# Attention followed by a mixture of experts on one core: how first and second layers are given out beside the attention steps

## The chip, the cores and the metric

The kernel runs on one core of a Trainium2 chip. The metric is the device time of one execution in microseconds (us). Before the change the median of three runs was 1072.3 us (1069.99 to 1074.8).

A core has five engines with an instruction stream of their own, each executed in order: TensorE (PE) for matrix products, VectorE (DVE), ScalarE (ACT), GpSimd (POOL) and SyncE (SP). They wait for one another through semaphores. SP and POOL issue nearly all DMA transfers. Matrix products are written to PSUM, from which DVE or ACT read them; everything else is held in SBUF.

## The reference

Two stages. The first is causal sliding-window attention with a distance bias (`q`, `k`, `v` are 8 batches x 8 heads x 576 tokens x 64):

```
scores = scale * q @ k.T                       # per batch and head
mask   = (rel >= 0) & (rel < 128)              # rel = query position - key position
scores = where(mask, scores - slope[h] * |rel|, -1e9)
attn   = softmax(scores);  x = attn @ v        # x: 4608 tokens x 512
```

The second is a dense mixture of 8 experts on the 4608 rows of `x`:

```
logits = x @ w_gate;  P = exp(logits - logits.max())
8 times: P /= P.sum(1) + 1e-9;  P /= P.sum(0) + 1e-9;  P *= 4608 / 8
out = sum over e of  P[:, e] * (relu(x @ w1[e]) @ w2[e])     # 512 -> 1024 -> 512
```

The gate needs all tokens before `P` is known, but the two layers of an expert need only the tokens of one group. So experts 0 and 1 are computed while the attention runs, and their results wait in `acc16` until `P` is there.

## The kernel before

**Attention in steps.** A batch has 576 tokens, five query blocks of 128 (`NQB`, the last one with 64). A step is (batch b, query block kb, half hf): four heads of one block. There are 8 x 5 x 2 = 80 steps. Each has four pieces:

- `scores` (L319): four products of 64 rows (head size) into `psS`, of which there is one buffer. Two heads lie in rows 0 to 63 and 64 to 127 of `QT` and `KT`, so these products use half of PE's rows each. Then on DVE a predicated copy (L338, not for kb = 0), which folds the window's two key blocks into one, and four bias-and-minimum operations (L349) that read `psS` out; on ACT four exponentials (L360).
- `normed` (L370): on DVE the reciprocal of the sums (L373, L377) and a multiplication (L378).
- `turned` (L385): four transposes on PE (L392) into `psT` (one buffer), a copy to SBUF on ACT (L401), and on DVE a masked copy `pto` (L415) and, once per block, the difference `dV` of two value blocks (L408).
- `values` (L423): value products (L437, L448) into `psX` (one buffer). Each writes 64 of PE's columns, two heads beside each other. After the second half ACT writes the block into `xT` (L457).

In iteration n of the main loop the pieces belong to different steps: scores of step n, `normed` of n-1, `turned` of n-2, `values` of n-3. `front` calls a piece with a priority raised by 600, so that the planner, which orders the instructions of DVE, ACT, POOL and SP, prefers it. PE's order is the order of the program (`manual_schedule`).

**Work between the pieces.** `run_fill(1)` puts one unit of the experts' work on PE. A unit is either a first layer (`l1_tile`, L191: 4 products of 384 columns, evicted by ACT at L198) or a whole second layer of a block of 128 tokens (`l2_tile`, L206: 8 products of 512 columns, evicted by DVE at L475). A job (expert e, token group g of 384) has eight of the one and three of the other. `woven` deals the second layers of the job before among the first layers of the next. An iteration calls `run_fill(1)` three times: behind the scores, behind the transposes, behind the values. First layers alternate between two `psh` buffers, second layers between two `psy` buffers.

**What comes in.** Rows of `q` and `k` come in per batch by POOL's queue (`load_qk`, L266), 576 KB each in short pieces; DVE permutes them (`spread`, L273), SP writes them to DRAM (L283), and two transposing transfers (`stage`, `turn`, L289 and L290) bring them back as `QT` and `KT`. `ahead` says at which step `spread` of the batch bb is called, and `early` at which step `load_qk(bb + 1)` is; `load_v` brings the values in block by block. Loads on POOL's queue are held behind a marker (L589) that waits for the newest block of `xT`. For batch 2 the order is `load_qk(2)` at step (1,0,0), `spread(2)` and `stage(2)` at (1,2,0), and in the same step's second half `load_qk(3)`.

**Behind the attention.** `gate` (L464) runs at the end of each batch. The normalisation of `P` (L711 to L739, DVE and POOL) begins when the last gate is there. Meanwhile PE works off the remaining jobs (L757 to L758), then experts 2 to 7 run in loops that the change does not touch.

Of the kernel before, what the change touches and what calls it, by code (L numbers as in the profile page):

```python
# [12 lines left out]
FP32 = mybir.dt.float32  # L13
# [3 lines left out]
def kernel(  # L17
# [10 lines left out]
    nc = tc.nc  # L28
# [5 lines left out]
    HD = H * Dh  # L34
# [150 lines left out]
    def new_hs(e, g):  # L185
        return [t[:, i, :] for t in h_tiles(per, "h", f"h_{e}_{g}") for i in range(4)]

    def l1_tile(e, ft, hs, t0, c0, c1, ps_pool, bufs=2):
# [9 lines left out]
        recent["act"] = nc.scalar.activation(  # L198
            out=hs[ft][:, c0:c1], in_=psh[:, c0:c1], func=AF.Relu
        )  # L200

    def l2_tile(e, blk, hs, ps_pool, bufs):
        psy = ps_pool.tile([P, HD], FP32, name=f"psy_{e}_{blk}", tag="psy", bufs=bufs)
        ms = blk % BG
        for ft in range(NFT):
            nc.tensor.matmul(  # L206
                out=psy,
                lhsT=hs[ft][:, P * ms : P * ms + P],
                rhs=w2ts[e][ft],
                start=(ft == 0),  # L210
                stop=(ft == NFT - 1),
            )
        return psy

    def woven(l1, l2):
        k = 0
        for i, u in enumerate(l1):
            if i % 2 == 0 and i > 0 and k < len(l2):
                yield l2[k]
                k += 1  # L220
            yield u
        yield from l2[k:]

    aps_scope = ExitStack()
    aps = aps_scope.enter_context(tc.tile_pool(name="aps", bufs=1, space=bass.MemoryType.PSUM))
    with tc.tile_pool(name="asb", bufs=1) as asb:
# [51 lines left out]
        def load_qk(b):  # L278
            nats[b] = [load_rows(q, b), load_rows(k, b)]
# [190 lines left out]
                    )  # L470
            nc.vector.tensor_copy(out=P_sb[:, b0:b1, :], in_=psG[:, 0 : b1 - b0, :])

        def l2_early(e, blk, hs):
# [12 lines left out]
        def early_job(e, g):  # L486
            hs = new_hs(e, g)
            return (
                [lambda ft=ft: l1_tile(e, ft, hs, GT * g, 0, GT, aps) for ft in range(NFT)],
                [lambda ms=ms: l2_early(e, BG * g + ms, hs) for ms in range(BG)]  # L490
                if g < NG - 1 or e == 0
                else hs,
            )

        jobs: list = []

        ready: list = []
        owed: list = []

        def run_fill(n):  # L500

            while n > 0:
                if not ready:
                    if jobs:
                        l1, l2 = early_job(*jobs.pop(0))
                        ready.extend(woven(l1, owed))
                        owed[:] = l2
                    else:
                        return
                ready.pop(0)()  # L510
                n -= 1

        new_T(0)

# [55 lines left out]
        t_next = v_next = 0  # L570
        for n in range(len(steps) + 3):
            lag = 1 if n < 2 else 2
            if n == 1:
# [3 lines left out]
            if n < len(steps):  # L577
# [7 lines left out]
                with ExitStack() as pin:  # L585
# [7 lines left out]
                    if hf == 1 and b + 1 < B and kb > 0:  # L593
                        load_v(b + 1, kb - 1)
                        if kb == NQB - 1:
                            load_v(b + 1, kb)
            front(scores, n)
            run_fill(1)
            front(normed, n - 1)
            if t_next <= n - lag:  # L600
                front(turned, t_next)
                t_next += 1
            run_fill(1)
            if v_next > n - lag - 1:
                continue
            front(values, v_next)
            run_fill(1)
            b, kb, hf = steps[v_next]
            v_next += 1
            if hf == 0:  # L610
                continue
            if b == 0 and kb < BG:
                ready += [
                    lambda ft=ft, kb=kb: l1_tile(0, ft, hs00, 0, P * kb, P * kb + P, aps)
                    for ft in range(NFT)
                ]
                ready.append(lambda kb=kb: l2_early(0, kb, hs00))
            done = b * S + min(S, (kb + 1) * P)
            while (g0 + 1) * GT <= done:

# [5 lines left out]
                jobs.append((1, 0))  # L626
            if kb == NQB - 1:
                g1 = S * (b + 1) // P
                gate(gate_done, g1)
                gate_done = g1  # L630

# [122 lines left out]
        if p < 2:  # L754
            nc.sync.dma_start(out=xps[2, p][:, 3:7, :], in_=slab(p))
    load_w2(2)
    while jobs or ready:  # L757
        run_fill(1)  # L758
    aps_scope.close()

# [343 lines left out]
```

## Time and profile before

| what | value |
|---|---|
| median of three runs | 1072.3 us |
| the profiled execution | 1069.8 us, span 1068.0 us |
| PE busy | 1022.8 us (96%) |
| DVE, ACT, POOL busy | 748.3, 657.9, 487.8 us |
| granted TensorE clock, mean | 0.994 |
| attention: first scores to last gate | 11.9 to 341.4 us |
| remaining jobs of experts 0 and 1 | 341.3 to 386 us |
| experts 2 to 7 | 386.6 us to the end |

PE is counted as busy from a product's start to its modelled end, and neighbouring products overlap in the records; how long a piece really holds PE is read from the starts of consecutive pieces. A wait is the idle time of an engine before an instruction, put down to what ended it. Times inside the trace count from the start of the span.

### The profile page before, as it was taken

To read this page: it belongs to the slowest core of one execution; us is meant where nothing else is said; L and a number is where in the kernel's file an instruction comes from. 1 tells how busy PE (TensorE), PEld (TensorE's weight loads), DVE (VectorE), ACT (ScalarE), POOL (GpSimd) and SP (SyncE) were. 2 spreads that over 40 slices of the span, in tenths; PEclk is the share of its full clock that TensorE was granted. 3 is DMA by queue.
4 is the path that set the end of the run, shared out by engine and by line. 5 is a ranking of instruction groups with operands and counts; after the bars stand their busy time and mean duration, and the time that the engine had idled before them with its cause. 6 is when DMAs were issued, how large, how long until landed. Compare 5 with 4: busy or idle time off the path is not lost.

```text
span 1068.0 us, 21178 instructions
## 1 busy us (share of the span) xinstructions
PE 1022.8 (96%) x7604; PEld 646.2 (61%) x7604; DVE 748.3 (70%) x1988; ACT 657.9 (62%) x1903; POOL 487.8 (46%) x420
## 2 busy tenths in 40 slices
PE   3788999999999989999999999999999999999998
PEld 2443444444445544555577777777777777777775
DVE  5886888887886866765466755775677657665565
ACT  4785877877876356664555555556555555555552
POOL 5321222111110200000677777777777877676760
PEclk9998999999999999999999999999999999999999
DMA  9999999524201944413432252315331452214443
GB/s 180 207 176 140 168 165 137 61 28 63 19 2 50 289 98 97 151 52 100 117 77 98 73 144 71 104 55 150 84 101 56 120 116 60 97 52 155 140 141 129
DMA packets 141258, 115.49 MB, mean 108 GB/s; under 512 B 73568, under 2 KB 130912, under 8 KB 141152
## 3 DMA queue, kind: packets, MB, share of 16 engines
q1 hardware_dynamic: 77664, 82.93, 26.4%
q0 software_dynamic: 63488, 31.21, 23.8%
q8 instruction: 59, 0.97, 0.4%
q14 instruction: 47, 0.39, 0.1%
HBM read 109.28 MB, written 25.95 MB: 127 GB/s over the span
## 4 chain that ended last, share of the span: by engine, by line
PE 81%; DVE 7%; ACT 5%; DMA 3%; issue 2%; POOL 1%; ACTq 0%; POOLq 0%; DVEq 0%
PE a L929 18%; PE psP L785 17%; PE psV L785 8%; PE psh L191 8%; PE psy L206 8%; PE b L929 7%; PE z L883 6%; PE psW L785 4%; ACT pc L360 2%; DMA acc<-in_k_dram 2%; PE psS L332 1%; DMA kT<-k 1%; PE psT L392 1%; PE psX L437 1%; DVE ts L349 1%
## 5 line engine op out<-in xcount | busy, mean ns | idle before, releaser
L191 PE MATMUL psh<-xT,w 128*128 128x384 f16 (+1 forms) x832 | 161.2, 321 | 7.5 <-ACT h L198 6.5
L929 PEld LDWEIGHTS <-h 128*128 128x128 f16 x1392 | 136.1, 98 | 50.0 <-POOL h L858 0.4
L806 ACT COPY psW<-psP 128x384 f32<-128x384 f32 x143 | 66.2, 463 | 148.5 <-PE psP L785 147.6
L857 POOL TENSOR_TENSOR xT<-h,h 128x768 f16<-128x768 f16 x58 | 95.1, 1640 | 120.8 <-DVE h L764 109.6
L785 PE MATMUL psP<-x,xT 128*128 128x384 f16 x576 | 140.6, 326 | 1.8 <-ACT u L770 1.5
L785 PE MATMUL psP<-x,w 128*128 128x384 f16 x576 | 140.7, 326 | 0.9 <-ACT h L198 0.6
L198 ACT ACTIVATE h<-psh 128x384 f16<-128x384 f32 (+1 forms) x208 | 93.4, 463 | 77.1 <-PE psh L191 75.9
L785 PEld LDWEIGHTS <-w 128*128 128x128 f16 x1152 | 112.6, 98 | 45.1 <-issue 2.3
L360 ACT ACTIVATE pc<-ts,nm 128x128 f16<-128x128 f32 (+1 forms) x320 | 124.9, 395 | 20.3 <-DVE nm L349 17.4
L206 PE MATMUL psy<-w,h 128*128 128x512 f16 x552 | 131.2, 380 | 2.5 <-DVE acc L475 2.2
L589 POOL COPY mark_sb<-xT 1x1 f16<-1x1 f16 x75 | 21.9, 293 | 235.9 <-ACT xT L457 229.5
L692 DVE SCALAR_TENSOR_TENSOR acc<-a,P_sb,acc 128x512 f32<-128x512 f32 x87 | 65.1, 748 | 85.3 <-PE a L929 85.3
L764 DVE CUSTOM_DVE_ANT_0 h<-psV,u 128x384 f16<-128x384 f32 x144 | 79.6, 553 | 58.2 <-PE psV L785 46.8
L785 PEld LDWEIGHTS <-xT 128*128 128x128 f16 x864 | 84.5, 98 | 39.1 <-issue 6.4
L929 PE MATMUL a<-xT 128*128 128x256 f16 x696 | 104.4, 273 | 0.0
L191 PEld LDWEIGHTS <-w 128*128 128x128 f16 x832 | 68.8, 99 | 55.6 <-issue 19.2
L858 POOL TENSOR_TENSOR h<-h 128x768 f16<-128x768 f16 x58 | 97.8, 1685 | 4.5
L859 POOL TENSOR_TENSOR xT<-h,xT 128x768 f16<-128x768 f16 x58 | 99.3, 1713 | 0.0
L855 POOL TENSOR_TENSOR s_sb<-h,xT 128x768 f16<-128x768 f16 x58 | 95.2, 1642 | 4.2
L940 DVE SCALAR_TENSOR_TENSOR acc<-a,P_sb,acc 128x256 f32<-128x256 f32 x174 | 82.8, 476 | 14.1 <-PE a L929 14.1
L929 PE MATMUL a<-w,h 128*128 128x256 f16 x636 | 91.7, 273 | 0.1
L883 PE MATMUL z<-w,h 128*128 128x512 f16 x360 | 90.6, 379 | 0.0
(96 smaller groups left out, 1951.1 us busy)
## 6 DMA issues: line engine op xcount, KB each, us to landing
x<-x SPq DMA_DIRECT2D x34, 1344.0 KB, 6.4
w<-in_moe_w_dram POOLq DMA_DIRECT2D x32, 512.0 KB, 7.2
out_dram<-acc SPq DMA_DIRECT2D x36, 256.0 KB, 2.0
x<-xT SPq DMA_DIRECT2D x8, 768.0 KB, 7.7
V<-in_v_dram POOLq DMA_DIRECT2D x32, 128.0 KB, 6.5
acc<-in_q_dram POOLq DMA_DIRECT2D x7, 576.0 KB, 8.7
acc<-in_k_dram POOLq DMA_DIRECT2D x7, 576.0 KB, 13.8
q<-acc SPq DMA_DIRECT2D x7, 576.0 KB, 4.2
```

Source lines behind the costliest of these rows:

```text
L191: nc.tensor.matmul(out=psh[:, c0:c1], lhsT=w1ts[e][dt][:, P * ft : P * ft + P], rhs=xT[:, dt, t0 + c0 : t0 + c1], start=(dt == 0), stop=(d ...
L198: recent["act"] = nc.scalar.activation(out=hs[ft][:, c0:c1], in_=psh[:, c0:c1], func=AF.Relu)
L206: nc.tensor.matmul(out=psy, lhsT=hs[ft][:, P * ms : P * ms + P], rhs=w2ts[e][ft], start=(ft == 0), stop=(ft == NFT - 1),)
L360: nc.scalar.activation(out=pc[0:nq, hh, :], in_=ts[0:nq, hh, :], func=AF.Exp, scale=-1.0, bias=nm[0:nq, hh : hh + 1], accum_out=den[0:nq, ...
L785: nc.tensor.matmul(out=ps, lhsT=a[:, kt, i, :], rhs=x[:, kt, :], start=start and kt == 0, stop=stop and kt == KH - 1, skip_group_check=True,)
L855: nc.gpsimd.tensor_tensor(out=s4, in0=a12, in1=s2, op=ALU.subtract)
L857: nc.gpsimd.tensor_tensor(out=s3, in0=a11, in1=a21, op=ALU.subtract)
L858: nc.gpsimd.tensor_tensor(out=a21, in0=a21, in1=a22, op=ALU.add)
L859: nc.gpsimd.tensor_tensor(out=s2, in0=a22, in1=s3, op=ALU.subtract)
L883: nc.tensor.matmul(out=psy, lhsT=hs(ft)[:, lo : lo + P], rhs=w2ts[e][ft], start=(ft == 0), stop=(ft == NFT - 1),)
L929: nc.tensor.matmul(out=ps, lhsT=a[ft], rhs=x[:, ft, :], start=start and ft == 0, stop=ft == NFT // 2 - 1, skip_group_check=True,)
L940: nc.vector.scalar_tensor_tensor(out=o, in0=ps, scalar=P_sb[:, blk, e : e + 1], in1=o, op0=ALU.mult, op1=ALU.add,)
```

## The change

It touches the attention part alone. The number and shapes of the products do not change: 577,536 columns of first- and second-layer products are issued before experts 2 to 7, in both kernels.

1. Second layers are issued in two halves of four products each (`l2_early` with `half`), into one `psy` buffer; the eviction follows the second half.
2. First layers and halves stand in two queues. `run_unit` takes a half when enough first layers lie behind it (`behind`) and `share`, which grows by 0.75 with each first layer and falls by 1 with each half, has reached a bound.
3. From step 10 on (`lead`, the end of batch 0's ten steps), `run_fill(fill)` gives out columns and not units: 0.96 x (8 x 4 x 384 + 3 x 8 x 512) / 11 = 2145 columns a call, with what was overdrawn kept in `count["left"]`. Before step 10 a call runs one unit, and a further half where one is open.
4. The third call stands before the value products, no longer behind them; and from step 10 on the scores of step n + 1 are issued directly behind the value products of iteration n, with no unit between.
5. `front` raises the priority only for steps below 10.
6. `gate` is called in the next iteration, behind its first fill.
7. `spread(3)` moves from step (2,0,0) to (2,1,0) and `load_qk(4)` with it, from (2,0,1) to (2,1,1); `load_qk(3)` moves from (1,2,1) to (1,4,0).

```diff
-            psy = l2_tile(e, blk, hs, aps, 2)
+        def l2_early(e, blk, hs, st, half):
+            if half == 0:
+                st.append(aps.tile([P, HD], FP32, name=f"psy_{e}_{blk}", tag="psy", bufs=2))
+            psy = st[0]
+            lo = P * (blk % BG)
+            for ft in range(NFT // 2 * half, NFT // 2 * (half + 1)):
+                nc.tensor.matmul(
...
+            if half == 0:
+                return
             recent["dve"] = nc.vector.tensor_copy(
...
+        def run_unit(half=False):
+            if not firsts_q and jobs:
+                start_job(*jobs.pop(0))
+            late = half or (
+                halves_q
+                and count["run"] >= halves_q[0][0]
+                and count["share"] >= (2 if count["whole"] else 1)
+            )
+            if halves_q and (late or not firsts_q):
+                halves_q.pop(0)[1]()
+                count["share"] -= 1
+                return NFT // 2 * HD
+            if firsts_q:
+                firsts_q.pop(0)()
+                count["run"] += 1
+                count["share"] = min(count["share"] + 0.75, 2.0)
+                return NDT * GT
+            return 0
         def run_fill(n):
...
+            if count["whole"]:
+                if run_unit() and halves_q and len(halves_q) % 2:
+                    run_unit(True)
+                return
+            count["left"] += n
+            while count["left"] > 0:
+                done = run_unit()
+                if not done:
+                    count["left"] = 0.0
+                    return
+                count["left"] -= done
...
+        lead = 2 * NQB
         def front(fn, n):
             if 0 <= n < len(steps):
-                with tc.high_priority(offset=600):
+                with tc.high_priority(offset=600 if n < lead else 0):
                     fn(*steps[n])
...
-        ahead = {(0, 2): 1, (1, 2): 2, (2, 0): 3, (2, 3): 4, (3, 1): 5, (3, 3): 6, (4, 1): 7}
+        ahead = {(0, 2): 1, (1, 2): 2, (2, 1): 3, (2, 3): 4, (3, 1): 5, (3, 3): 6, (4, 1): 7}
...
-                early.setdefault((b, kb, 1) if b else (1, 0, 0), []).append(lambda bb=bb: load_qk(bb + 1))
+                early.setdefault({1: (1, 0, 0), 2: (1, 4, 0)}.get(bb, (b, kb, 1)), []).append(lambda bb=bb: load_qk(bb + 1))
...
+        fill = 0.96 * (NFT * NDT * GT + BG * NFT * HD) / 11
...
-            front(scores, n)
-            run_fill(1)
+            count["whole"] = n < lead
+            if n < lead:
+                front(scores, n)
+            run_fill(fill)
+            if gates:
+                gate(*gates.pop())
             front(normed, n - 1)
             if t_next <= n - lag:
                 front(turned, t_next)
                 t_next += 1
-            run_fill(1)
+            run_fill(fill)
             if v_next > n - lag - 1:
                 continue
+            run_fill(fill)
             front(values, v_next)
-            run_fill(1)
+            if n + 1 >= lead:
+                front(scores, n + 1)
```

More of the change, by code (lines that the diff above doesn't have):

```diff
@@ L200, in l1_tile @@
         )
[L202 to L222, printed above, removed]
     aps_scope = ExitStack()
@@ L484, in l2_early @@
                 store_x(NP - 2, slab(2)[:, 0:3, :])
-        def early_job(e, g):
-            hs = new_hs(e, g)
[L488 to L492, printed above, removed]
-            )
-        jobs: list = []
-        ready: list = []
-        owed: list = []
-        def run_fill(n):
[L502 to L511, printed above, removed]
+        jobs: list = []
@@ new lines, with add_halves, add_firsts @@
+        owed: list = []
+        firsts_q: list = []
+        halves_q: list = []
+        count = {"queued": 0, "run": 0, "share": 0.0, "left": 0.0, "whole": True}
+        def add_halves(e, blk, hs, behind):
+            st: list = []
+            for half in range(2):
+                halves_q.append(
+                    (count["queued"] + behind, lambda half=half: l2_early(e, blk, hs, st, half))
+                )
+        def add_firsts(units):
+            firsts_q.extend(units)
+            count["queued"] += len(units)
@@ L612 @@
             if b == 0 and kb < BG:
[L613 to L617, printed above, removed]
+                add_firsts(
+                    [
+                        lambda ft=ft, kb=kb: l1_tile(0, ft, hs00, 0, P * kb, P * kb + P, aps)
+                        for ft in range(NFT)
+                    ]
+                )
+                add_halves(0, kb, hs00, 1)
             done = b * S + min(S, (kb + 1) * P)
@@ L628 @@
                 g1 = S * (b + 1) // P
[L629 removed]
+                gates.append((gate_done, g1))
                 gate_done = g1
+        gate(*gates.pop())
     ssb = ctx.enter_context(tc.tile_pool(name="ssb", bufs=1))
@@ L756 @@
     load_w2(2)
-    while jobs or ready:
+    while jobs or firsts_q or halves_q:
         run_fill(1)
```

14 lines of the change are left out of this document (13 added, 1 removed).

## The prediction

> **What bounds the kernel now.** I read the page first: how full each engine is, then the slices.
>
> ```profile
> PE 1022.8 (96%) x7604; PEld 646.2 (61%) x7604; DVE 748.3 (70%) x1988; ACT 657.9 (62%) x1903; POOL 487.8 (46%) x420
> ...
> PE   3788999999999989999999999999999999999998
> ...
> PEclk9998999999999999999999999999999999999999
> DMA  9999999524201944413432252315331452214443
> ```
>
> PE is busy 96% of the span. What is missing lies in the first four slices (26.7 us each), where DMA is full and the clock dips once. So the change can gain in three ways only: PE stands less, PE's clock stays up, or the same products hold PE for less time. Next, PE's waits in two windows, 40 to 102 us and then 102 to 340 us.
>
> ```profile
> PE psS L332 <- DMA kT<-k: 3.4, 1, 3.4
> PE psS L332 <- DVE nm L349: 3.1, 5, 1.0
> PE psh L191 <- ACT h L198: 2.2, 4, 1.1
> ...
> PE psh L191 <- ACT h L198: 3.7, 5, 1.3
> PE psS L332 <- DVE nm L349: 0.2, 1, 0.2
> ```
>
> In batches 2 to 7 (the last two lines) PE waits only 3.9 us in 238. Batch 1 and the step into batch 2 are dearer: the keys of batch 2 come 3.4 us late. The table by stretches shows what that does (columns: stretch, its length, busy time of PE, PEld, DVE, ACT, POOL, clock, DMA share, GB/s):
>
> ```profile
> 82.00:85.00 3.00, 1.26 (x6) 0.39 (x4) 1.03 (x4) 1.16 (x6) 0.00 (x0) 1.00 1.56 225
> 85.00:88.00 3.00, 1.34 (x8) 0.60 (x8) 0.90 (x9) 0.51 (x3) 0.00 (x0) 0.59 0.65 41
> 88.00:91.00 3.00, 2.74 (x18) 1.17 (x17) 2.75 (x8) 1.74 (x8) 0.00 (x0) 0.50 0.00 0
> 91.00:94.00 3.00, 2.19 (x10) 0.81 (x10) 0.79 (x5) 1.63 (x4) 1.90 (x4) 0.50 0.94 281
> 94.00:97.00 3.00, 3.00 (x15) 1.15 (x13) 1.87 (x11) 2.40 (x10) 0.00 (x0) 0.70 0.70 140
> ```
>
> After the wait the clock is at half for some nine microseconds. Busy time times missing clock is the price: 1.34 x 0.41 + 2.74 x 0.50 + 2.19 x 0.50 + 3.00 x 0.30 = 3.9 us. Last, PE's timeline in a steady step (start, length, instruction):
>
> ```profile
> 233.47 0.25 PE L437 MATMUL psX<-pto,dV 128*64 128x128 f16 x2
> 233.55 0.22 PE L448 MATMUL psX<-pt,V 128*64 128x128 f16 x2
> 233.61 0.22 PE L437 MATMUL psX<-pto,dV 128*64 128x128 f16 x2
> 233.66 0.22 PE L448 MATMUL psX<-pt,V 128*64 128x128 f16 x2
> 233.82 0.82 PE L191 MATMUL psh<-xT,w 128*128 128x384 f16 x4
> 234.57 0.39 PE L332 MATMUL psS<-kT,qT 64*128 64x256 f16 x4
> 234.90 0.82 PE L191 MATMUL psh<-xT,w 128*128 128x384 f16 x4
> 235.56 0.39 PE L392 MATMUL psT<-ident,pc 128*128 128x128 f16 x4
> 235.78 1.89 PE L206 MATMUL psy<-w,h 128*128 128x512 f16 x8
> ```
>
> The starts tell. A first layer in front of the transposes, which use the whole array as it does, holds PE 0.66 us (234.90 to 235.56); in front of the scores 0.75 (233.82 to 234.57): 0.09 more. The full array streams 384 x 4 columns in about 0.65, so 0.42 ns a column. The scores stream 4 x 256 columns two at a time, 0.21 us, and hold PE 0.33: 0.12 more. The values stream 8 x 128 two at a time, 0.21, and hold it 0.35: 0.14 more. Every change of the array's shape costs 0.09 to 0.14 us. A step has four.
>
> **The change, part by part.** *Scores next to values (point 4).* Counted over PE's planned order, neighbours of different shape fall from 347 to 274: 73 fewer. What stood between values and scores cost 0.14 + 0.09 = 0.23 us in two changes; now there is one, from two column halves to two row halves. No row shows that pair without a wait. If it is free, the gain is 73 x 0.23 = 16.8 us; if it costs as much as both, nothing; at worst 0.34, a loss of 8. I take one ordinary change of 0.13, the nearest row being the 0.14 with which values end: a gain of 0.10 x 73 = 7.3 us. [...]
>
> *Load of batch 3 later (point 7).* In the trace POOL issues it at 63.2 and 65.2 us, SP the transposes of batch 2 at 65.6 and 74.0; SP needs 8.3 and 9.0 us to issue them, against 2.6 each at 35 us, and the keys land at 86.5. At the new place, the marker at 73.0, the load of 1.15 MB starts about ten microseconds later. With SP's issue back near 2.6 us the keys' transfer starts near 68.5 and with its 12.5 us lands near 81; PE wants it at 83.3 or later. So the 3.4 us and the 3.9 us of slow clock go: -7.3 us; bounds 0 (transfer still late) and -8.4 (the 1.1 us wait at 91 too). What is late next is the load itself: it took 8.7 and 16.0 us, so landing by 82 and 90; DVE's permutation (L273, which blocks everything behind it on DVE) is moved from step (2,0,0) to (2,1,0), two steps of 3.7 behind 83.3, 91. It fits by a microsecond; if not, DVE's wait stops the scores too. On POOL's queue it passes two value loads of batch 2, which start earlier for it, and markers of 0.2 us. `load_qk(4)`, one block later, lies beside the transposes of batch 3 as it does now (issued at 92.3, transposes from 94.7 us), and those are wanted a batch of 36 us after batch 2's: 0, at most the same 7 us if that cover is gone.
>
> *Columns given out (points 2 and 3).* Counted in the planned order, up to the first scores of batch 2 66,560 columns are issued instead of 58,368: 8192 x 0.42 ns = 3.4 us of PE work is brought forward into batch 1, where PE waits. Batch 1 took 36.2 us before the late keys (47.07 to 83.26); PE's pieces in it sum to 30.3 (columns at 0.42 ns, shape changes at 0.11), afterwards to 32.7. If it lasts as long as before, 3.4 us are gained; if the waits stay whole, 1.0; I take the middle, 2.2. For batches 2 to 7 the steps become shorter: 3.87 us of PE pieces on average before, 3.64 after, of which 0.07 to 0.11 is the shape changes; the rest is only given to the jobs behind the attention (105,000 columns behind the last gate, some 44 us) and gains nothing by itself.
>
> *Halves (point 1).* Same columns, and DVE's eviction (0.61 us from start to start) still comes once per block: 0 us; behind the attention the two `psy` buffers wait 2.2 us for DVE today, bounds -2 to +2. *Gate later (6):* 0, its 0.5 us on PE only moves.
>
> *No priority (point 5).* Nothing of work changes, only the planner's order on DVE and ACT. From start to start a full step costs DVE 0.60 (predicated copy) + 4 x 0.21 + 0.40 (L373, L377) + 0.60 (L378) + 0.34 (`pto`) + 0.17 (half a `dV`) + 0.8 x 0.61 = 3.4 us. Over the planned order, permutations included (0.9 each), batches 2 and 3 average 3.51 a step, batches 4 to 7 3.2. Against PE's 3.64 that is 96% and 88%, where it was 91% and 83%. ACT needs 4 x 0.385 + 0.47 + 2.1 x 0.38 + 0.24 = 3.1. PE's first-layer evictions now stand between exponentials in ACT's order and no longer behind all four, which speaks against the `psh` waits (3.7 us); DVE's fullness speaks for new `psS` waits. Bounds: -4 (all present waits go) to +20 (0.33 us a step, below); I take +1, that is waits of some 5 us in place of 3.9.
>
> Sum: -7.3 - 7.3 - 2.2 + 1 = -15.8 us. The profiled execution took 1069.8 (span 1068.0), 2.5 below the median; 1054 for it, and **1056.5** against the median of 1072.3.
>
> **The rivals.** *A, DVE becomes the bound, slower.* There is one `psS`, and scores n + 1 may not start before the last L349 of step n. Before, that L349 ends at 237.06 and the next scores start at 238.71: 1.65 us of slack in a step of 4.13. A step of 3.65 leaves 1.2. Without priority an eviction (0.61), a normalisation (0.60) and a `dV` (0.34) can stand ahead of the predicated copy: 1.55, so PE waits 0.35 in such a step. It decides where waits exceed 16.8 us over 60 steps, 0.28 a step. At 0.55 a step: 1072.3 - 16.8 + 33 = 1088. For it: 96% in batches 2 and 3, and a stretch of 5.8 us of DVE work between two score readings in batch 1's planned order (4.0 before). Against: those 5.8 are followed by 2.3, and the mean does not rise.
>
> *B, the keys stay late.* The transposes are slow from their own short pieces, not the load: the 7.3 us stay, 1064. For it: value loads share the window. Against: 2.6 us a transpose elsewhere.
>
> *C, scores behind values cost as much as with work between:* 1064 as well.
>
> *D, PE's clock falls again and again.* The one 3.4 us wait cost 3.4 + 3.9; once per batch in six batches +44 us less the gain, 1100. Waits up to 1.3 us left the clock at 1.00 from 102 to 340, so it needs A at its worst. [...]
>
> **How the numbers follow.** About 0.5%, 5.4 us, is what a measurement of this kernel can tell from no change. My case 0.58 (1048 to 1066); B or C alone 0.16 (1060 to 1068); waits that eat most of the gain 0.10 (1067 to 1077); A 0.13 and D 0.03 (1078 and more). Faster: 0.58 + most of 0.16 = 0.72; same 0.12; slower 0.16. The range 1046 to 1077 leaves out A and D, and the corner where every bound is good. My case's own range is 1048 to 1066.
>
> **What would show it.** In the changed profile: scores start about 0.35 us behind the values' start with no product between, and the next product 0.33 later (point 4); no wait for `kT` near 84 us and a clock of 1.00 in every slice from 40 us on (point 7); the last gate near 322 us (340.8 before) and the first product of expert 2 near 371 (386.6); `psS` waits for L349 below 6 us in batches 2 to 7. Wrong would be: `psS` waits of over 15 us there, a wait of DVE at the permutation for its load, or a clock below 0.95 in any later slice.

## The result, and the profile after

The changed kernel takes 1058.4 us (median; 1054.4 to 1063.5), the kernel before 1072.1 (1070.0 to 1075.0): a ratio of 0.987 [0.984, 0.990], 13.7 us less. Forecast were 1056.5 us and a range of 1046 to 1077, with 15.8 us less. The sum came out; several of its terms did not.

The profiled execution of the changed kernel is its longest, 1063.45 us with a span of 1061.7, so it shows less of the gain than the median: 6.3 us of span. The page, PE's busy time and the slices (PE, PE's clock, DMA):

```profile
PE 1013.9 (95%) x7604; PEld 650.4 (61%) x7604; DVE 743.6 (70%) x1988; ACT 657.2 (62%) x1903; POOL 480.3 (45%) x420
...
PE   3489899999999989999999999999999999999998
...
PEclk9989999999999999999999999999999999999999
DMA  9998999435203844315431352225331542214343
```

The same 7604 products hold PE 8.9 us less than before. But the third slice (53 to 80 us) shows a clock below full, which was forecast away. PE's waits, first from 40 to 102 us, then from 102 to 340 (columns: in total, times, longest):

```profile
PE psS L310 <- DMA kT<-k: 6.8, 1, 6.8
PE psh L191 <- ACT h L198: 2.5, 5, 1.1
PE psS L310 <- DVE nm L327: 1.6, 3, 0.7
PE psh L191 <- ACT xT L435: 0.4, 1, 0.4
...
PE psS L310 <- DVE nm L327: 3.9, 2, 2.5
PE psh L191 <- ACT xT L435: 0.9, 1, 0.9
```

The five `psh` waits for ACT's evictions in batches 2 to 7 (3.7 us before) are gone; two `psS` waits have come. And there is a wait for keys of 6.8 us, twice as long as before, but at another place. PE's timeline there:

```profile
47.41 0.22 PE L426 MATMUL psX<-pt,V 128*64 128x128 f16 x2
54.45 0.40 PE L310 MATMUL psS<-kT,qT 64*128 64x128 f16 x4 [6.82 <-DMA kT<-k]
```

These are the first scores of batch 1. The keys of batch 2, for which PE waited before, now arrive in time: its first scores start at 94.44 with no idle time. During the wait, from 50.2 us on, the clock (the third figure from the end) falls to 0.50, as it did before:

```profile
49.00:52.00 3.00, 0.00 (x0) 0.00 (x0) 0.00 (x0) 0.19 (x2) 2.75 (x5) 0.69 1.56 126
52.00:55.00 3.00, 0.55 (x7) 0.39 (x8) 0.12 (x1) 0.00 (x0) 0.00 (x0) 0.50 1.64 152
55.00:58.00 3.00, 3.00 (x20) 1.64 (x18) 2.13 (x13) 2.13 (x10) 0.00 (x0) 0.50 1.25 207
58.00:61.00 3.00, 3.00 (x22) 1.17 (x22) 1.20 (x10) 1.74 (x7) 0.35 (x2) 0.60 1.76 181
```

Busy time by missing clock, that is 0.55 x 0.5 + 3.00 x 0.5 + 3.00 x 0.4 = 3.0 us. With the wait, 9.8 us hang on keys that the kernel before had in time. The other executions, up to 9 us shorter, cannot all have paid that.

A steady step (PE's timeline), values, scores, next product:

```profile
77.74 0.25 PE L415 MATMUL psX<-pto,dV 128*64 128x128 f16 x2
77.82 0.22 PE L426 MATMUL psX<-pt,V 128*64 128x128 f16 x2
77.88 0.22 PE L415 MATMUL psX<-pto,dV 128*64 128x128 f16 x2
77.93 0.22 PE L426 MATMUL psX<-pt,V 128*64 128x128 f16 x2
78.09 0.39 PE L310 MATMUL psS<-kT,qT 64*128 64x256 f16 x4
78.41 0.82 PE L458 MATMUL psy<-w,h 128*128 128x512 f16 x3
```

From values to scores 0.35 us, from scores on 0.32: within a hundredth of the 0.35 and 0.33 that were forecast. Less 0.21 us each, the estimate for 1024 columns two at a time at 0.42 ns, the values still pay 0.14 at their end and the scores 0.11 at theirs; what has gone is the entry into the scores, 0.09.

**A balance of PE's time.** The experiments are read with a table in which all runs are treated alike. "Waits" is the sum of PE's waits up to 400 us. "Clock" is busy time by missing clock, summed over stretches of 3 us from 10 to 400 us. "Own work" is the span less both. "Changes" counts neighbours of different array shape in the planned order. Below, "the copy" is the changed kernel unaltered, profiled once more.

| kernel | median | span | waits | clock | own work | changes |
|---|---|---|---|---|---|---|
| before | 1072.1 | 1068.0 | 39.3 | 5.4 | 1023.3 | 347 |
| changed | 1058.4 | 1061.7 | 42.2 | 3.0 | 1016.5 | 274 |
| copy | 1059.7 | 1058.7 | 37.1 | 3.2 | 1018.4 | 274 |
| scores apart again | 1063.1 | 1061.5 | 35.5 | 2.9 | 1023.1 | 344 |
| before, point 4 alone | 1072.4 | 1069.5 | 46.7 | 3.6 | 1019.2 | 278 |
| before, point 7 alone | 1071.7 | 1069.4 | 40.8 | 5.4 | 1023.2 | 347 |
| point 7 undone | 1055.6 | 1054.5 | 33.3 | 3.4 | 1017.8 | 274 |
| priority throughout | 1066.8 | 1069.3 | 46.4 | 6.5 | 1016.4 | 274 |
| halves issued together | 1068.1 | 1066.9 | 44.3 | 5.8 | 1016.8 | 274 |
| best, at the end | 1053.8 | 1052.0 | 33.8 | 3.0 | 1015.2 | 274 |

PE's own work falls into two groups: 1023.1 to 1023.3 with 344 and more changes of shape, 1015.2 to 1019.2 with 274 or 278. Four later versions that the table leaves out, all with 274 changes, lie at 1016.3 to 1018.3. Two profiles of the same kernel (changed, copy) differ by 1.9. So about 6 us of the gain are the changes of shape (4 to 8 by the spread of the rows), and the rest of what separates these kernels is waits and clock.

### The profile page after: what moved, and what is told of

It reads as the page before. It is cut to its first block, busy times and chain, and to the rows that moved or that the text cites. A ratio compares the mean times of both kernels' runs of the same rounds, so it can differ in the third digit from the quotient of the medians.

```text
span 1061.7 us, 21168 instructions
## 1 busy us (share of the span) xinstructions
PE 1013.9 (95%) x7604; PEld 650.4 (61%) x7604; DVE 743.6 (70%) x1988; ACT 657.2 (62%) x1903; POOL 480.3 (45%) x420
## 4 chain that ended last, share of the span: by engine, by line
PE 84%; DMA 5%; DVE 4%; ACT 2%; issue 2%; POOL 2%; SPq 0%; POOLq 0%; ACTq 0%; DVEq 0%
PE a L971 18%; PE psP L827 17%; PE psy L458 9%; PE psh L191 9%; PE psV L827 9%; PE b L971 7%; PE z L925 7%; PE psW L827 4%; DMA acc<-in_k_dram 2%; PE psS L310 2%; DMA acc<-in_q_dram 1%; DMA kT<-k 1%; PE psT L370 1%; PE psX L415 1%; ACT pc L338 1%
## 5 line engine op out<-in xcount | busy, mean ns | idle before, releaser
L191 PE MATMUL psh<-xT,w 128*128 128x384 f16 (+1 forms) x832 | 153.6, 319 | 3.8 <-ACT h L198 2.5
L458 PE MATMUL psy<-w,h 128*128 128x512 f16 x552 | 141.5, 383 | 1.5 <-DVE acc L467 1.5
L827 PEld LDWEIGHTS <-w 128*128 128x128 f16 x1152 | 112.6, 98 | 45.6 <-issue 2.7
L621 POOL COPY mark_sb<-xT 1x1 f16<-1x1 f16 x75 | 16.3, 217 | 231.6 <-ACT xT L435 230.8
L191 PEld LDWEIGHTS <-w 128*128 128x128 f16 x832 | 74.0, 100 | 58.1 <-issue 12.4
```

What stands on the lines that cost most here:

```text
L191: nc.tensor.matmul(out=psh[:, c0:c1], lhsT=w1ts[e][dt][:, P * ft : P * ft + P], rhs=xT[:, dt, t0 + c0 : t0 + c1], start=(dt == 0), stop=(d ...
L458: nc.tensor.matmul(out=psy, lhsT=hs[ft][:, lo : lo + P], rhs=w2ts[e][ft], start=(ft == 0), stop=(ft == NFT - 1),)
L827: nc.tensor.matmul(out=ps, lhsT=a[:, kt, i, :], rhs=x[:, kt, :], start=start and kt == 0, stop=stop and kt == KH - 1, skip_group_check=True,)
```

## The experiments

**The copy.** Is the 6.8 us wait part of the changed kernel, or of one execution? The file is the changed kernel as it is.

> The changed kernel once more, for a second profile. In its first profile (1063.5 us, the longest of six executions) the keys of batch 1 came 6.8 us late and the clock then stood at half for some six microseconds, together about 9.7 us; in the profile of before there was no such wait. Theory, that this wait is a race of the transposing transfers with the weights of expert 1 and falls out differently from execution to execution: this profile has another wait at the first scores of batch 1, between 0 and 7 us, its span is 1052 to 1062 us, and span minus (wait and slow clock) is near 1052 again. Rival, that the change itself makes these keys late: the wait is 6 to 8 us again, and the span about 1061.

Measured 1059.7 us (1057.9 to 1061.4), ratio 0.990 [0.986, 0.993], span 1058.7, and no wait for keys. The two medians of this one kernel, 1058.4 and 1059.7, differ by 1.3 us, so differences of that size say nothing below. What differs is when two issues meet. In the changed kernel's profile SP starts the transposing transfer of batch 1's keys 0.30 us before POOL issues the first-layer weights of expert 1. SP's timeline, then POOL's:

```profile
36.39 3.62 SPq L267 DMA_TRANSPOSE qT<-q  x1
40.06 2.93 SPq L268 DMA_TRANSPOSE kT<-k  x1
...
40.36 1.40 POOL L108 DMA_DIRECT2D w<-in_moe_w_dram  x2 [0.29 <-issue]
```

In the copy they are 0.82 us apart (38.45, 39.27), before 0.67 (37.95, 38.62); with priority throughout 0.44, and there the keys came 6.7 us late. From SP's start to its landing the transfer took 14.3 us in the late case, 7.7 in the kernel before. By these profiles it is a race of two queues, and the changed kernel can lose it. That the short distance is what makes the keys late was not tried by setting it: in the late profile the transfer of `q` had already taken SP 3.62 us before the weights were issued, against 2.64 in the kernel before and 2.67 in the copy.

The copy has waits of its own. Batch 2's keys, still in natural order, arrive 2.0 us late at DVE's permutation, at 63.58, and PE then waits 2.7 us for `psS` at 66.63; at 118.25 it waits 2.55 behind the permutation of batch 4. The clock around these two:

```profile
67.00:70.00 3.00, 2.67 (x15) 1.47 (x14) 2.60 (x13) 3.00 (x14) 1.06 (x3) 0.65 1.04 160
70.00:73.00 3.00, 3.00 (x20) 1.10 (x18) 0.71 (x2) 1.29 (x5) 0.16 (x1) 0.78 1.30 162
118.00:121.00 3.00, 2.75 (x16) 1.51 (x17) 3.00 (x12) 2.27 (x11) 0.71 (x2) 0.68 1.71 335
121.00:124.00 3.00, 3.00 (x21) 1.28 (x21) 2.11 (x12) 2.50 (x10) 2.06 (x4) 0.75 0.90 163
```

**Point 4 undone: scores apart from values again.**

```diff
-            run_fill(fill)
+            if n < lead - 1:
+                run_fill(fill)
             front(values, v_next)
             if n + 1 >= lead:
+                run_fill(fill)
                 front(scores, n + 1)
```

> The changed kernel with the third call of run_fill back between the value products and the next scores; all else stays. Changes of the array's shape rise from 274 to 344. Theory, that each costs 0.09 to 0.10 us of PE: 6.3 to 7.0 us longer than the changed kernel, about 1065, and the hold of scores behind a first layer is 0.09 us more than a first layer alone again. Rival, that what is won there is waited for elsewhere: within 2 us of the changed kernel.

Measured 1063.1 (1062.1 to 1065.5), ratio 0.993 [0.991, 0.995], 3.4 above the copy. The fifty steps of batches 3 to 7, from the gate of batch 2 to that of batch 7, take 189.39 us against the copy's 184.70: 0.094 a step, the entry into the scores. The balance has the same 4.7 us in own work. The price stands. The time lies between the theory and the rival: waits and clock are 1.9 us less than in the copy, which would fit the rival in part, but they differ by 4.9 between the two profiles of the changed kernel, so that this share is waited for elsewhere is not shown.

**Point 4 alone, on the kernel before.**

```diff
-            front(scores, n)
+            if n < 2 * NQB:
+                front(scores, n)
             run_fill(1)
...
-            front(values, v_next)
-            run_fill(1)
+            if n + 1 >= 2 * NQB:
+                run_fill(1)
+                front(values, v_next)
+                front(scores, n + 1)
+            else:
+                front(values, v_next)
+                run_fill(1)
```

> The kernel before with one thing of the change: from step 10 on the third unit stands ahead of the value products and the next scores directly behind them; raised priority, whole units and load times stay. Changes of the array's shape fall from 347 to 278. Theory, that each is worth 0.094 us of PE (what batches 3 to 7 of the run with scores apart showed): 6.5 us shorter than before, about 1066, with the late keys of batch 2 as long as before or longer, since batch 1 does no more work. Rival, that the gain is only had together with the lowered priority: within 3 us of before.

Measured 1072.4, ratio 1.0005 [0.9994, 1.0016]: nothing. Own work falls by 4.1 us in the balance, but PE's waits from 102 to 340 us rise from 3.9 to 8.2:

```profile
PE psh L191 <- ACT h L198: 6.2, 7, 1.6
PE psS L332 <- DVE nm L349: 1.5, 2, 1.0
PE psG L464 <- ACT xT L457: 0.5, 1, 0.5
```

and the keys of batch 2 come 6.0 us late in place of 3.4. PE saves time on its products and then stands for as long. The rival's time came; its reason, that the gain needs the lowered priority, was not tried.

**Point 7 undone: loads and permutation of batch 3 at their old places.**

```diff
-        ahead = {(0, 2): 1, (1, 2): 2, (2, 1): 3, (2, 3): 4, (3, 1): 5, (3, 3): 6, (4, 1): 7}
+        ahead = {(0, 2): 1, (1, 2): 2, (2, 0): 3, (2, 3): 4, (3, 1): 5, (3, 3): 6, (4, 1): 7}
...
-                early.setdefault({1: (1, 0, 0), 2: (1, 4, 0)}.get(bb, (b, kb, 1)), []).append(lambda bb=bb: load_qk(bb + 1))
+                early.setdefault((b, kb, 1) if b else (1, 0, 0), []).append(lambda bb=bb: load_qk(bb + 1))
```

> The changed kernel with the three loads and permutations back at their old steps (load of batch 3 at (1,2,1), permutation of batch 3 at (2,0,0), load of batch 4 at (2,0,1)). Theory, that the load of batch 3 made the keys of batch 2 late: a wait of 2 to 5 us for kT at the first scores of batch 2 and a clock at half behind it, 5 to 8 us lost, less the 2.5 us wait behind the permutation of batch 4, which goes: 3 to 6 us longer, about 1062. Rival, that the work brought forward into batch 1 (8192 columns, 3.4 us) would hide the keys anyway: no wait there, and 2 us shorter, about 1056.

Measured 1055.6 (1053.7 to 1056.3), ratio 0.986 [0.983, 0.989]: 4.1 us below the copy and 2.8 below the first six runs of the changed kernel: the rival's time. SP's timeline, and PE's at the first scores of batch 2:

```profile
64.80 3.83 SPq L267 DMA_TRANSPOSE qT<-q  x1
68.73 7.83 SPq L268 DMA_TRANSPOSE kT<-k  x1
...
87.54 0.22 PE L426 MATMUL psX<-pt,V 128*64 128x128 f16 x2
87.69 0.29 PE L310 MATMUL psS<-kT,qT 64*128 64x128 f16 x4
```

SP's issue is as slow beside the load as before (7.8 us). Yet PE does not wait for these keys, because they land at 85.2 (16.5 us behind SP's start) and it comes for them at 87.7 and not at 83.3: by the trace 66,560 columns of first and second layers lie ahead of these scores, and 58,368 in the kernel before, so 8192 more. And without point 7 the load of batch 4 is not late: the 2.5 us wait near 118 and the clock behind it are gone. So in the changed kernel point 7 buys nothing that points 2 and 3 do not already give, and costs 3 to 4 us.

**Point 7 alone, on the kernel before.** The two lines of the diff of the change for `ahead` and `early`, nothing else.

> The kernel before with only the three load and permutation steps of the change. Theory, that the later load does free the keys of batch 2, but that in the changed kernel they would have been in time anyway: here no kT wait at the first scores of batch 2, no half clock behind it, 7 us gained, less 2 to 4 us behind the permutation of batch 4, which waits for its load: about 1067. Rival, that the load has no part in the keys' lateness: a kT wait of 3 us again and 1072 to 1075.

Measured 1071.7, ratio 1.0005 [0.9993, 1.0017]. The waits from 40 to 102 us, first line, and from 102 to 340:

```profile
PE psS L332 <- DVE nm L349: 3.1, 5, 1.0
...
PE psS L332 <- DVE nm L349: 4.3, 2, 4.1
PE psh L191 <- ACT h L198: 3.4, 4, 1.3
```

Here the forecast mechanism is seen alone: no wait for keys, the first scores of batch 2 at 84.29, and from 40 to 102 us waits and clock come to 6.0 us less than before (8.4 against 14.4). From 102 to 340 us they come to 6.4 more: 4.1 us of waiting behind the permutation of batch 4, whose load starts a block later, and a slow clock behind that. A gain and its bill, equal; the theory had put the bill at 2 to 4 us.

**Point 5 undone: priority throughout.**

```diff
-                with tc.high_priority(offset=600 if n < lead else 0):
+                with tc.high_priority(offset=600):
```

> The changed kernel with the raised priority in all steps. Theory, that the priority costs or brings little because DVE's and ACT's work is the same and PE is the bound: within 3 us of the changed kernel, with psS waits for L327 and psh waits for ACT between 2 and 9 us from batch 2 on. Rival, that giving it up was what let the shorter steps run without waits: 10 us longer or more, with psh or psS waits of over 12 us.

Measured 1066.8 (1064.0 to 1071.1), ratio 0.995 [0.993, 0.998]: 7 us above the copy. Waits of PE from 102 to 340 us:

```profile
PE psS L310 <- DVE nm L327: 5.1, 2, 3.9
PE psh L191 <- ACT h L198: 3.0, 8, 0.9
PE psh L191 <- ACT xT L435: 0.3, 1, 0.3
```

The `psh` waits are back, eight of them, and in batch 1 they are 5.0 us against 2.5 in the changed kernel. With priority a first layer's eviction stands behind all four exponentials of a step (ACT at 203.27 to 204.73 us, each with 0.39 and 0.19 for the reading of its sum), without it between them. The time lies between theory and rival. Late keys do not explain it, since even the fastest of ten runs, 1064.0, is above the slowest of the changed kernel, 1063.5. Against the changed kernel's profile, which had late keys too, the span is 7.6 us longer: 5.5 more of `psh` waits for ACT's `h`, 1.2 more of `psS` waits from 102 us on (DVE stood 4.14 us for the rows of batch 4, not 2.36), 3.5 more of slow clock, less 2.6 in other rows. Of the clock 1.4 lies ahead of 40 us, where both kernels have the same priority. So the `psh` waits are the part that the priority explains; the rest is not shown to come from it.

**Point 1 undone: the two halves issued together.**

```diff
                 halves_q.pop(0)[1]()
-                count["share"] -= 1
-                return NFT // 2 * HD
+                halves_q.pop(0)[1]()
+                count["share"] -= 2
+                return NFT * HD
```

> The changed kernel with both halves of a second layer issued together, so 4096 columns in one piece. Theory, that halving is free and brings nothing but evenness: within 2 us of the changed kernel (1058 to 1060). Rival, that the even steps are what keeps DVE's and ACT's answers in time: psS and psh waits of over 8 us in batches 2 to 7 in place of some 5, and 1064 or more.

Measured 1068.1 (1064.1 to 1068.8), ratio 0.996 [0.994, 0.997]: 8.4 us above the copy: the rival's time. Waits of PE from 40 to 102 us, first line, then from 102 to 340:

```profile
PE psh L191 <- ACT h L198: 8.1, 6, 4.2
...
PE psS L310 <- DVE nm L327: 4.6, 4, 2.4
PE psh L191 <- ACT h L198: 2.5, 5, 1.3
PE psh L191 <- ACT xT L435: 1.7, 2, 1.5
```

A whole second layer is 4096 columns, a call gives out 2145. After it a call is skipped or two first layers come at once, and then PE fills both `psh` buffers and stands before the third until ACT has emptied one: at 62.52 eight first-layer products in a row, the next at 68.21. PE's timeline, then ACT's:

```profile
68.21 0.81 PE L191 MATMUL psh<-xT,w 128*128 128x384 f16 x4 [4.23 <-ACT h L198]
...
66.14 0.40 ACT L338 ACTIVATE pc<-ts,nm 128x128 f16<-128x128 f32 x1 [2.67 <-DVE nm L327]
```

This longest wait is not the bunch's alone. ACT's exponentials, which stand ahead of the eviction, waited 2.67 us for DVE, and DVE had stood at the permutation of batch 2 for rows that were late (1.95 us at 60.93, 1.50 at 64.08). In the copy the same rows were 2.0 us late and cost PE 2.7, as a `psS` wait. From 102 to 340 us, where DVE waits for no rows, waits and clock come to 12.1 us against the copy's 5.6, and 4.2 of it are `psh` waits, of which the copy has none. So the bunches show there; how much of the 8.4 us is theirs was not measured.

**Permutations later (on the changed kernel).** If the load of batch 4 is what DVE waits for, its permutation can come later instead of the load earlier.

```diff
-        ahead = {(0, 2): 1, (1, 2): 2, (2, 1): 3, (2, 3): 4, (3, 1): 5, (3, 3): 6, (4, 1): 7}
+        ahead = {(0, 2): 1, (1, 2): 2, (2, 1): 3, (2, 4): 4, (3, 2): 5, (3, 4): 6, (4, 2): 7}
```

> The changed kernel with the permutations of batches 4 to 7 one query block later (and the loads behind them with them); nothing else. Theory, that the permutation of batch 4 stands on DVE before its load has landed (2.4 us of DVE's wait, 2.5 of PE's, and in one profile a slow clock behind it): no DVE wait for that load, no psS wait of over 1 us in batch 2, and 2.5 to 4 us shorter than the changed kernel, 1055 to 1057. Rival, that the load of batch 4 lands later too, because something else fills the queues: the wait stays over 1.5 us, and the time within 1.5 us of the changed kernel.

Measured 1055.1 (1052.9 to 1058.7), ratio 0.985 [0.983, 0.988]. From 102 to 340 us PE waits 1.7 us in all and the clock is at 1.00. That is the cost of point 7 shown from its other side, as the theory had it. The keys of batch 1 were 1.0 us late and the `psS` wait of 2.1 us at 66.28 stayed.

**Weights of expert 1 a block later (on the kernel with point 7 undone).**

```diff
-            (0, 3, 1): [lambda: load_w1(1)],
-            (0, 4, 1): [lambda: load_w2(1)],
+            (0, 4, 1): [lambda: load_w1(1)],
+            (1, 0, 1): [lambda: load_w2(1)],
```

> The changed kernel with the load steps of before (as in the run e3_loads, 1055.6) and the weights of expert 1 loaded later: first layer's at (0,4,1), second layer's at (1,0,1). Theory, that the weights of the first layer, when POOL issues them within half a microsecond of the transposes of batch 1, make those keys late, and that the other weights delay the rows of batch 2: no kT wait at the first scores of batch 1, the permutation of batch 2 waits under 1 us for its load (1.4 before), 1051 to 1055. Rival, that the moved weights come late themselves: a wait of PE for DMA at the first job of expert 1 or at its first second layer, and 1056 or more.

Measured 1055.7 (1055.1 to 1056.7), ratio 0.986 [0.984, 0.987]: as without the edit. The keys of batch 1 are in time, but PE waits 1.8 us for the weights at 71.20 and 1.7 for the keys of batch 2 at 90.23, so the late weights of the rival came. The wait moves with the transfer.

**Three versions towards a better kernel.** All have the later permutations. The first also permutes a batch's q and k one step apart, transposes in the second half of the block, and issues both weight loads of expert 1 at (0, 4, 1):

```diff
-        def spread(b):
-            for nat, dst in zip(nats.pop(b), (q16s[b], k16s[b])):
+        def spread(b, which=(0, 1)):
+            for i in which:
+                nat, dst = nats[b][i], (q16s[b], k16s[b])[i]
...
-            (0, 3, 1): [lambda: load_w1(1)],
-            (0, 4, 1): [lambda: load_w2(1)],
+            (0, 4, 1): [lambda: load_w1(1), lambda: load_w2(1)],
...
-                if hf == (0 if b else 1):
+                if b or hf:
                     if (b, kb) in ahead:
                         with tc.issue_after(recent["dve"].ins):
-                            spread(ahead[b, kb])
-                    if kb == 2 and b + 1 < B:
+                            spread(ahead[b, kb], (hf,) if b else (0, 1))
+                    if hf and kb == 2 and b + 1 < B:
                         stage(b + 1)
```

> The changed kernel with all waits for transfers taken on: permutations of batches 4 to 7 one block later; the two permutations of a batch a step apart, the transposes in the second half of their block; both weights of expert 1 at (0,4,1). Theory, that what the changed kernel still loses in batches 1 and 2 are these waits (2.7 us behind the two permutations of batch 2 and a slow clock behind it, 2.5 us behind those of batch 4, the keys of batch 1 in some executions) and no lack of DVE time: no psS wait over 1.2 us from 50 us on, clock 1.00 in all stretches there, 1050 to 1054, and a narrower spread than 1054 to 1063. Rival, that DVE is full in these batches and the waits move elsewhere: 1056 or more, with new psS or psh waits of 2 us or more.

1057.5 (1057.2 to 1060.0), ratio 0.988 [0.985, 0.990]. From 102 to 340 us PE waits 0.8 us; but both weights now go ahead of batch 2's rows, DVE waits 4.2 us for these at 64.81 and PE 3.8 at 67.87. So the time and the new wait are the rival's, but late rows made it and not a full DVE. The second puts the weights back to (0, 3, 1) and (0, 4, 1):

> The copy with the permutations of batches 4 to 7 one block later (e7_permute), a batch's q and k permuted in different steps of the block with the transposes in its second half (e11_timed), and expert 1's weights back at their old places, (0,3,1) and (0,4,1). Theory: in e11_timed the 3.8 us wait near 68 us came from both weight loads standing together ahead of batch 2's rows. With the second ones a block apart again, as in e7_permute, DVE's wait for batch 2's rows falls from 4.2 us to 2 at most, PE's psS wait at 60 to 70 us is 1.2 us or less, the clock is 1.00 in 60 to 80 us, and the time is 1051 to 1054. Rival: the weights at (0,3,1) meet the transposes of batch 1 again, a kT wait of 1 to 7 us shows at 47 us, and the time is 1055 or more.

1053.8 (1050.8 to 1056.3), ratio 0.983 [0.980, 0.986], the lowest median measured, though the 1055.1 of the later permutations and the 1054.3 of the next version are no more than 1.3 us above it. DVE's wait for batch 2's rows is 0.9 us. PE's waits, from 40 to 102 us and, in the last line, the longest row from 102 to 340:

```profile
PE psh L191 <- ACT h L198: 2.6, 4, 1.1
PE psS L311 <- DVE nm L328: 1.4, 3, 0.7
PE psh L191 <- ACT xT L436: 1.0, 2, 0.5
PE psS L311 <- issue: 0.8, 1, 0.8
...
PE psS L311 <- DVE nm L328: 3.1, 3, 1.8
```

The clock is at 1.00 from 60 us on. A late load is left all the same: at 140.63 DVE waits 2.57 us for the rows of batch 5. In the profiled execution the transpose was 1.1 us ahead of the weights. The third moves the first-layer weights one step earlier, to (0, 3, 0), to take them out of the race:

> As e12_apart, but the first-layer weights of expert 1 are issued one step earlier, at (0,3,0). Theory: what makes the keys of batch 1 late is that these weights are issued within half a microsecond of SP's first transpose of batch 1. Issued a step (about 2 us or more) earlier, they are ahead of the transposes in every execution: no kT wait at 47 us, runs that differ by less than 3 us, time 1050 to 1054. Rival: it is the traffic of the weights as such and not the moment of issue that slows the transposes; then a kT wait of 1 us or more shows at 47 us whichever comes first, and the time is 1055 or more.

1054.3 (1052.6 to 1056.2), ratio 0.984 [0.981, 0.986], but PE waited 2.5 us for the keys of batch 1. The rival's wait came, its time of 1055 or more did not, and the runs differ by 3.6 us where the theory had less than 3. With the weights on the move, the rows of `k` took 4.5 us from SP's write to the first transpose (33.61 to 38.08; 2.0 in the version before it), and the transposes came late by that. So the half microsecond of the theory is not all that makes these keys late: here the weights were issued 14.6 us ahead of the transpose of `k` (27.91 and 42.52). Where they would disturb nothing was not found.

## Why the prediction was right, and where it was not

**The total** is right with four of its terms off: they happen to cancel, so much of the hit is luck. Undone one at a time, points 4, 5 and 1 are worth 3.4, 7.1 and 8.4 us, and point 7 costs 3 to 4. These need not add up to the gain, since each was undone with the others in place; points 2, 3 and 6 were not tried alone.

Of the three signs of being wrong, two came: DVE waited at a permutation for its load, and the clock was below 0.95 in the slice from 53 to 80 us. The third, `psS` waits of over 15 us, did not: they were 3.9.

**Scores next to values (point 4): right.** Predicted 7.3 us from 0.10 for each of 73 changes; measured 0.094 a step, and 6.3 us in the balance (mean own work of the six rows with 274 changes 1016.9, of the three with 344 and more 1023.2). The 0.35 us from values to scores, 0.14 above the estimate for the columns, say that the one change left between them still costs the 0.14 with which the values ended before. Neither a free neighbourhood (16.8 us) nor rival C (nothing) came. What the prediction did not see is that the gain is only worth something if nothing else becomes late for it: alone it gave 0.

**Later load of batch 3 (point 7): the step failed.** "So the 3.4 us and the 3.9 us of slow clock go: -7.3 us" holds on the kernel before (6.0 us measured from 40 to 102 us). In the changed kernel the 8192 columns brought into batch 1 already let the keys come in time: the term was counted for a cover that the other term supplied. And "`load_qk(4)`, one block later [...] 0" was wrong, since only its effect on SP's transposes was asked. It is the load that is late, by 2.4 us, and DVE's permutation of batch 4 (`spread(4)`, unmoved) waits for it with the score readings behind it:

```profile
121.00 0.96 DVE L251 COPY acc<-acc 96x3072 f16<-96x3072 f16 x1 [2.36 <-DMA acc<-in_k_dram]
```

The forecast looked for this at batch 3, where it fitted, and not at batch 4. Net of both, point 7 costs 3 to 4.

**Columns given out (2 and 3): their effect was in another place.** The -2.2 us for batch 1 cannot be seen: from its first scores to those of batch 2 it lasts 40.0 us in the changed kernel, 41.5 in the copy and 40.5 with point 7 undone, against 36.2 before and 39.6 with the late keys. So it grew by all of the 3.4 us of work and some slow clock, and the waits inside it were not filled. What the work filled was the wait for the keys, which the forecast had given to point 7. These points were not tried alone.

**Halves (point 1): "0 us", measured 8.4** by issuing them together. The forecast counted columns and evictions, and not that a unit of twice a call's columns makes first layers come in bunches on two `psh` buffers. The `psh` waits from 102 us on show the bunches; the longest one, at 68.21, has late rows in it as well.

**No priority (point 5): "+1", measured -7, of which 5.5 us are seen as `psh` waits.** The `psh` waits went as the prediction's own argument said (3.7 us before, 0 from ACT's `h` in batches 2 to 7 now); the new `psS` waits it set against them, 5 us for want of room on DVE, are not there. The 3.9 us of `psS` in the changed kernel are a late load (2.5) and two permutations in a row in front of the scores at 184.37 (1.5). Rival A is out: between its bounds of -4 and +20 the wrong end was weighed.

**Not foreseen: the keys of batch 1**, 9.8 us in the profiled execution. So the marks did not all hold: from batch 2's first scores (94.44) to the last gate (332.06) it takes 237.6 us, as forecast (84 to near 322), but this stretch starts ten microseconds late; the last gate is at 332.06 and not near 322, expert 2 at 380.3 and not near 371. In the best version they are at 322.2 and 370.4. Expert 2 to the end takes 681 to 682 us in every kernel. Rival B did not come for batch 2. Rival D's clock fell after late keys in the changed kernel's profile and after two `psS` waits in the copy's, 1.6 us each time there, and never once a batch.

## What to carry to other kernels

Price what a change saves on the busiest engine by instruction, but give it a value only together with what keeps that engine fed: scores next to values saved 3.4 us where the other parts stood beside them and nothing alone, and the parts priced at nothing or at a small loss, halves and priority, kept 7 to 8 us away. When a load is moved, follow it to its first reader and ask who stands behind that reader in its engine's order; the batch after the one that the move is for is the place to look. And compare whole balances, waits and clock and the rest, over several profiles, since one profile may hold a race that another does not.

## What was not expected of the hardware

**The slow clock comes in pieces of 3.4 us.** In stretches of 0.25 us the clock is 1.00 or 0.50 in the profiles of the two kernels, and in between only where it changes: 0.50 from 34.50 to 37.75 and from 85.75 to 95.75 us before, from 50.25 to 60.25 in the changed kernel. So missing clock times length over 0.5 is the time at half clock: in the copy (0.35 + 0.22) x 3 / 0.5 = 3.4 us, and again (0.32 + 0.25) x 3 / 0.5 = 3.4. In the kernel before, behind its late keys, (0.41 + 0.50 + 0.50 + 0.30) x 3 / 0.5 = 10.3, three pieces; in the changed kernel (0.31 + 0.50 + 0.50 + 0.40) x 3 / 0.5 = 10.3. The same sum gives about 3.4, 6.8 or 10.3 us for every slow stretch between 10 and 400 us in all fourteen profiles. With point 7 alone, where PE waited 4.1 us, there are two (0.35 + 0.50 + 0.28 gives 6.8):

```profile
115.00:118.00 3.00, 0.61 (x5) 0.20 (x6) 2.46 (x11) 1.20 (x7) 0.00 (x0) 0.65 1.63 156
118.00:121.00 3.00, 3.00 (x8) 1.08 (x9) 2.87 (x14) 2.43 (x10) 1.57 (x3) 0.50 1.39 349
121.00:124.00 3.00, 3.00 (x22) 1.49 (x20) 1.78 (x5) 1.97 (x8) 1.20 (x3) 0.72 1.15 173
```

The length of a wait did not tell whether a piece followed: a wait of 2.48 us behind batch 4's permutation left the clock at 1.00 in the changed kernel's profile, 2.55 us at the same place cost a piece in the copy, and in the kernel with point 7 undone even 1.46 us at 175.03 cost one (clock 0.78 and 0.65 in 175 to 181 us), where the same length at 184.37 in the changed kernel cost none. These waits are shorter than one piece. So of these waits of 1.5 to 2.5 us each cost itself, and then either nothing or, by missing clock, 1.6 to 1.7 us more. What decides was not shown.

**A transposing transfer was slow behind the issue of a load of rows.** In the profiles of the two kernels and at the keys of batches 2 and 3 in the one with point 7 undone, SP needs 6.7 to 8.9 us for each of the five that it begins within 4 us behind such an issue. In the first two it needs 2.3 to 4.2 us for each of the fourteen that have no such issue in the 13 us ahead of them or beside them. So the "2.6 us a transpose elsewhere" of the prediction is the pair at 35 us only; in the same profile the later ones, from 127 us on, took 2.3 to 5.8. The keys of batch 1 took 14.3 us from SP's start to landing when the weights were issued 0.30 us behind. In the eleven profiles where the weights were issued 0.67 us and more behind it they were at most 1.0 us late. What makes such a transfer slow was not shown.
